# A Strassen mixture-of-experts kernel: second matmuls held back by three pieces, the even chunk split behind its silu, and the first expert's tokens transposed block by block

## The chip, the cores and the metric

The kernel runs on one core of a Trainium2 chip. The metric is the device time of one execution in microseconds (us); shorter is better. Engines are named as the profile names them: PE (matmul) with its weight loads PEld, DVE (vector), ACT (scalar), POOL (GpSimd) and SP (the engine that issues most DMAs).

## The reference

For 2048 tokens of width 512, the output is the input, plus a linear-attention block, plus a mixture of eight experts of which each token uses two:

```python
xn = _layernorm(x)
return x + _A_ref(xn, A_wqkv, A_wo) + _B_ref(xn, B_w_gate, B_w1, B_w2)

# _A_ref: 32 heads of width 16, no mask
pq, pk = phi(q), phi(k)                      # phi(t) = (t + 1 if t > 0 else exp(t)) + 1e-6
kv, z = sum over s of pk^T v, sum over s of pk
o = (pq @ kv) / (pq . z + 1e-6);  return o @ wo

# _B_ref: E = 8, F = 1792, K = 2
logits = xf @ w_gate;  gates = softmax(top-2 logits)
for e in range(E):
    h = silu(xf @ w1[e]) @ w2[e]
    out += w_e * h                            # w_e: the token's gate for e, or 0
```

## The kernel before

**Stages.** Until about 104 us the kernel normalises the 16 token tiles, transposes them and projects the keys. Until about 206 us it projects the queries tile by tile (`q_proj`, L1122), applies the attention of tiles 0 to 10 (`o_proj`, L1167) and, in between on DVE, computes the routing (`routing`, in slices that `piece` and the loop pull out of a generator). From 206 to 967 us it runs the experts. Last it applies the attention of the five remaining tiles and adds them to the output.

**Precision.** Each fp32 operand is split into a high part (ACT copies to fp32r, L111) and a low part (DVE subtracts, L114); each matmul then takes three passes (high x high, high x low, low x high). So a matrix that ACT or DVE produced can be used by PE only when ACT's high part is there, and for the other passes when DVE's low part is.

**Experts and pairs.** The experts are sorted by load: `r` is the place, with capacities of 576 to 512 tokens. An expert's tokens are gathered from DRAM by POOL in blocks of 128 (`gather1`, L901, tile `xg`), transposed by PE (`x_block`, L927, tile `xep`), copied by ACT (L934, tile `xr`) and split. The hidden width 1792 is cut into seven pairs `j` of two chunks of 128 (an even and an odd one). All pairs but the first two use a Strassen scheme, `pair_fast`: seven products p0 to p6 (L1071) of six matmuls each. p0, p2, p4 and p6 accumulate in one PSUM tile `px`, p1 and p3 in `pz`, p5 in `py`; after each product ACT or DVE reads the running sum. These tiles come from the tag `mm`, which has two buffers. p5 completes the even chunk: DVE adds (L1102), ACT applies silu (L1103), then `h_split` makes the high and the low part of `h`. p6 completes the odd chunk (silu at L1108).

**Second matmul.** `mm2` (L999 and L1002) multiplies a chunk of `h` with `w2`. One call, three matmuls, is a *piece*: one chunk into one accumulator `d`. For r = 0 to 4 there are six accumulators, d = 0 and 1 for 256 tokens at full width (L999, 512 columns) and d = 2 to 5 with the rest of the tokens transposed (L1002, 272 to 320 columns); for r = 5 to 7 (capacity 512, "single") there are four of 512 columns. The pieces of a pair are dealt out while the *next* pair runs: `fill(k)` puts some ahead of product k, `jobs(k)` issues the weight and token preparation behind it. Weight sums (L842 to L846, tile `wr`), their high parts (`ws`, `wa`, `w`) and the next expert's token sums (L945) all sit in `jobs`.

**Order of the work.** The order of every engine's queue is that in which the code issues it; nothing is reordered afterwards. `plan(g)` fills the slots, and its list `front` holds what goes between the first pieces of a pair: the next expert's `x_block`s (at j = 2, 3, 4) and the transposed outputs of the expert before (`y_out`, at j = 1 and 2).

Of the kernel before, what the change touches and what calls it, by code (L numbers as in the profile page):

```python
# [48 lines left out]
NPLAIN = 2  # L49
# [9 lines left out]
def linear_attn_plus_moe(  # L59
# [26 lines left out]
    def ta(name, w=D, dt=F32):  # L86
        t = wp.tile([P, DX if dt == F32 else 2 * DX], dt, tag="a", name=name, bufs=11)
        return t[:, :w]
# [34 lines left out]
    def load_x(t):  # L123
        xt[t] = ta(f"x{t}")
        Q.dma_start(xt[t], x[t * P:(t + 1) * P, :])
# [471 lines left out]
    def piece(n=1):  # L597
        for _ in range(n):
            next(side)
# [164 lines left out]
    def mid_b():  # L764
        kvs = kvw["s"]
        for i in range(2):
            M_v.append(hilo(tb, f"M{i}", 2))
        for g in range(4):
            mp = psm("acc", f"mp{g}")
            for i, (a, b) in enumerate(PASSES):  # L770
                T.matmul(mp, kvs[:, a, g * P:(g + 1) * P], wo_v[g // 2][b][:, g % 2, :],
                         start=(i == 0), stop=(i == 2))
            split(M_v[g // 2][0][:, g % 2, :], M_v[g // 2][1][:, g % 2, :], mp)
            if g % 2:
                for h in range(2):
                    Q.dma_start(M_d[g // 2, h].rearrange("p (k f) -> p k f", k=2), raw(M_v[g // 2][h]))
# [102 lines left out]
    def single(r):  # L879
        return CAP[r] == 4 * P  # L880
# [5 lines left out]
    def by_token(r):  # L886
        return [0, 1, 2, 3] if single(r) else [0, 1]
# [8 lines left out]
    def gather1(r, i):  # L896
        if i == 4 and single(r):
            return
        b = r * RB + i
        t = ta(f"xg{r}_{i}", DX)  # L900
        G.indirect_dma_start(out=t, out_offset=None, in_=xn_d,  # L901
                             in_offset=IOA(ap=gidx[:, b:b + 1], axis=0))
        xg[r, i] = t
# [61 lines left out]
    def h_split(r, n, hs):  # L965
        split(*hh[r, n], hs)
# [50 lines left out]
    def nacc(r):  # L1017
        return 4 if single(r) else 2 + KC

    def pieces(r, j):  # L1020
        e, o = 2 * j, 2 * j + 1
        n = nacc(r)
        if j < NP - 1:
            order = [(e, d) for d in range(n)] + [(o, d) for d in range(n)]
        else:
            order = [(e, 0), (e, 1), (e, 2), (o, 0), (o, 1), (o, 2)]
            order += [(c, d) for d in range(3, n) for c in (e, o)]
        return [lambda c=c, d=d: mm2(r, c, d) for c, d in order]

    def y_out(r, k, tag="mm"):  # L1030
# [28 lines left out]
    def pair_fast(r, j, fill, jobs):  # L1059
        n = half(r)  # L1060
        he, ho = h_tiles(r, j)
        c11, c12 = he[:, :n], he[:, n:]
        c21, c22 = ho[:, :n], ho[:, n:]

        def product(k, ps_, start):
            wn, xn_ = PRODUCTS[k]
            which, o = WPOS[wn]
            w, x = W1[r, j][which], XF[r, xn_]
            for kc in range(2):
                for i, (a, b) in enumerate(PASSES):  # L1070
                    T.matmul(ps_, w[a][:, o + kc, :], x[b][:, kc, :],  # L1071
                             start=(start and kc == 0 and i == 0), stop=(kc == 1 and i == 2),
                             skip_group_check=True)

        fill(0)
        px = psm("mm", f"px{r}_{j}", n)
        product(0, px, True)
        A.activation(c11, px, AF.Copy)  # L1078
        jobs(0)
        fill(1)  # L1080
        pz_ = psm("mm", f"pz{r}_{j}", n)
        product(1, pz_, True)
        A.activation(c22, pz_, AF.Copy)
        jobs(1)
        fill(2)
        product(2, px, False)
        A.activation(c12, px, AF.Copy)  # L1087
        jobs(2)
        fill(3)
        product(3, pz_, False)  # L1090
        V.tensor_tensor(c12, pz_, c12, op=ALU.add)  # L1091
        A.activation(c12, c12, AF.Silu)  # L1092
        jobs(3)
        fill(4)
        product(4, px, False)
        V.tensor_tensor(c22, px, c22, op=ALU.add)  # L1096
        A.activation(c22, c22, AF.Silu)  # L1097
        jobs(4)
        fill(5)
        pz_ = psm("mm", f"py{r}_{j}", n)  # L1100
        product(5, pz_, True)
        V.tensor_tensor(c11, pz_, c11, op=ALU.add)  # L1102
        A.activation(c11, c11, AF.Silu)  # L1103
        jobs(5)
        fill(6)
        product(6, px, False)
        h_split(r, 2 * j, he)
        A.activation(c21, px, AF.Silu)  # L1108
        jobs(6)
        h_split(r, 2 * j + 1, ho)  # L1110


    zt = ta("zt")
# [5 lines left out]

    eq = {}  # L1120

    def q_proj(t):  # L1122
        qp = psm("mm", f"qp{t}")
        for kc in range(KC):
            for i, (a, b) in enumerate(PASSES):
                T.matmul(qp, xT(t, a, kc), wq_v[kc // 2][b][:, kc % 2, :],
                         start=(kc == 0 and i == 0), stop=(kc == KC - 1 and i == 2))
        e = ta(f"e_q{t}")
        A.activation(e, qp, AF.Relu, scale=-1.0)
        A.activation(e, e, AF.Exp, scale=-1.0)  # L1130
        A.activation(e, e, AF.Identity, bias=eps6)
        eq[t] = (qp, e)

    def q_feat(t):
        qp, e = eq.pop(t)
        pq[t] = ta(f"pq{t}")
        V.scalar_tensor_tensor(pq[t], qp, 0.0, e, op0=ALU.max, op1=ALU.add)
        pz[t] = ta(f"pz{t}")
        G.tensor_tensor(pz[t], pq[t], zb, op=ALU.mult)
# [6 lines left out]
    def q_den(t):  # L1146
        dens[t] = wp.tile([P, H], F32, tag="den", name=f"den{t}", bufs=2)
        V.tensor_reduce(dens[t], heads(pz[t]), axis=AX.X, op=ALU.add)
# [67 lines left out]
    mid_lo(0)  # L1216
    mid_sum(1)
    mid_lo(1)
    q_proj(2)
    piece()  # L1220
    q_feat(1)
    mid_b()
    load_x(0)
    q_transp(0)
    q_den(1)
    q_norm(1)
    q_feat(2)
    q_proj(3)
    q_den(2)
    q_norm(2)  # L1230
    load_x(1)
# [4 lines left out]
    for t in range(OLAG + 1, NT - 2):  # L1236
        if t < NO + OLAG:
            o_out(t - OLAG - 1)
        spent = 0.0
        while spent < PERIOD:  # L1240
            c = next(side, None)
            if c is None:
                break
            spent += c
        q_den(t - 1)
        if 8 <= t < 11:
            fetch_w()
        q_proj(t)
        q_norm(t - 1)
        if t > NO:  # L1250
            pz_out(t - 1)
        q_feat(t)
        if t == 4:
            Q.dma_start(out[NO * P:S, :], x[NO * P:S, :])
        if t < NO + 2:
            load_x(t - 2)
            q_transp(t - 2)
        if t >= 11:
            plain_w()
        if t - OLAG < NO - 1:  # L1260
            o_proj(t - OLAG)
        while late:
            late.pop(0)()
        if t in (11, 12):
            gather1(0, 2 * t - 22)
            gather1(0, 2 * t - 21)
        if t == 13:
            gather1(0, 4)
            x_block(0, 0)
            x_block(0, 1)  # L1270


    t = NT - 2
# [1 line left out]
    q_proj(t)  # L1275
    q_norm(t - 1)
    pz_out(t - 1)
    x_block(0, 2)
    x_block(0, 3)
    q_feat(t)  # L1280
    q_proj(t + 1)
    x_block(0, 4)
    for name in ("B11", "B21", "B12", "B22"):
        x_hi(0, name)
        x_lo(0, name)
# [8 lines left out]
    def plan(g):  # L1294
# [48 lines left out]
            for k, f, name in steps.get(j, ()):  # L1343
                on(k, f, r + 1, name)
        if r > 0 and not single(r - 1):
            tg = "tr" if single(r) else "mm"
            for k in {1: (0, 1), 2: (2,)}.get(j, ()):
                front.insert(0 if j == 2 else len(front), lambda k=k: y_out(r - 1, k, tg))
        if j == 3 and r in (E // 2, E - 1):
            on(0, G.drain)  # L1350
        if r == E - 1:
# [9 lines left out]
                        front.append(lambda k=k: q_transp(NO + 2 * (j - 4) + k))  # L1361
        return at, front

    for g, (r, j) in enumerate(pairs):
        at, front = plan(g)
        todo = pieces(*pairs[g - 1]) if g else []
        rest = []
        if g == len(pairs) - 1:
            todo, rest = todo[:4], todo[4:]
        slots_ = 4 if g < NPLAIN else 7  # L1370
        total = len(todo)
        first = min(total, 2 + len(front)) if g >= NPLAIN else total // 4
        share = [first + (total - first) * k // (slots_ - 1) for k in range(slots_)]
        emitted = [0]

        def fill(k):
            while k == 0 and front:
                if emitted[0] < total:
                    todo[emitted[0]]()
                    emitted[0] += 1  # L1380
                front.pop(0)()
            while emitted[0] < share[k]:
                todo[emitted[0]]()
                emitted[0] += 1

        def jobs(k):
            for f in at[k]:
                f()

        (pair_plain if g < NPLAIN else pair_fast)(r, j, fill, jobs)  # L1390
        assert emitted[0] == total
        if g == 0:
            q_den(NT - 1)
            q_norm(NT - 1)
            pz_out(NT - 1)
# [83 lines left out]
```

## Time and profile before

| | |
|---|---|
| median of 3 runs | 988.62 us (986.51 to 989.22) |
| the profiled execution | 991.18 us, of which the instructions span 989.2 us |
| PE busy | 897.1 us (91% of the span) |
| DVE busy | 667.5 us (67%) |
| ACT busy | 550.3 us (56%) |
| POOL busy | 177.4 us (18%) |
| mean granted PE clock | 0.978 |
| DMA | 108.84 MB, mean 110 GB/s |

The profile gives for each engine when an instruction ran, how long the engine was idle before it and which engine's event ended that idle time. A row of the timeline reads: start, duration, engine, line, operation, tile written and tiles read, shape, count, and in brackets the idle time and its releaser. Matmuls are pipelined and their ends are modelled: the pace of PE is read from start to start, not from the durations. ACT and DVE rows overlap a little for the same reason.

### The profile page before, as it was taken

The numbers are of one execution on the slowest core, as the hardware profiler recorded it, in microseconds if no ns is written. First come the engines' busy times: TensorE is split into PE (matmuls) and PEld (weight loads), VectorE is DVE, ScalarE is ACT, GpSimd is POOL, SyncE is SP. The second block draws the span as 40 slices with busy tenths as digits, with TensorE's granted clock in tenths as the row PEclk, the third lists the DMA queues.
The fourth block names the chain that finished last, engine by engine and source line by source line (L and its number), as shares of the span: only waits on it lengthen the run. The fifth ranks groups of instructions, "written<-read, shape, count | busy, mean of one in ns | idle before, by whom it ended". The sixth has DMA issues, their size and how long they took to land. (4 is left out here: it accounts for less than half of the span.)

```text
span 989.2 us, 15229 instructions
## 1 busy us (share of the span) xinstructions
PE 897.1 (91%) x5582; PEld 790.4 (80%) x5582; DVE 667.5 (67%) x1441; ACT 550.3 (56%) x1191; POOL 177.4 (18%) x200
## 2 busy tenths in 40 slices
PE   9999999899898989998898889988888889889996
PEld 8899877678788878887888778877777777777785
DVE  7888789876675666657665775566667665766641
ACT  5665443555556655665655556555655555555540
POOL 2532143731004100410041003100400130020002
PEclk9999999999999999999999999999999999999999
DMA  5531164624226322632263226222632362256306
GB/s 171 171 129 43 57 212 133 200 87 128 86 69 134 114 86 80 144 91 85 86 136 101 77 85 159 79 75 75 161 97 66 87 157 67 83 116 204 117 1 151
DMA packets 71183, 108.84 MB, mean 110 GB/s; under 512 B 7618, under 2 KB 37570, under 8 KB 71074
## 3 DMA queue, kind: packets, MB, share of 16 engines
q1 hardware_dynamic: 62402, 87.82, 28.2%
q0 software_dynamic: 7840, 18.57, 9.8%
q10 hardware_dynamic: 864, 1.44, 0.4%
q8 instruction: 45, 0.74, 0.3%
q14 instruction: 32, 0.26, 0.1%
HBM read 85.89 MB, written 23.24 MB: 110 GB/s over the span
## 5 line engine op out<-in xcount | busy, mean ns | idle before, releaser
L976 POOL DMA_INDIRECT out_dram<-yo,sidx x37 | 58.4, 1579 | 637.3 <-DVE yo L974 577.2
L114 DVE TENSOR_TENSOR h<-hs,h 128x512 fp32r<-128x512 f32 (+5 forms) x112 | 79.6, 711 | 47.1 <-ACT h L111 46.3
L1091 DVE TENSOR_TENSOR hs<-pz,hs 128x256 f32<-128x256 f32 (+5 forms) x54 | 23.4, 434 | 91.7 <-PE pz L1071 86.6
L111 ACT ACTIVATE h<-hs 128x512 fp32r<-128x512 f32 (+5 forms) x112 | 70.9, 633 | 0.2
L1078 ACT ACTIVATE hs<-px 128x256 f32<-128x256 f32 (+5 forms) x54 | 21.1, 392 | 84.7 <-PE px L1071 84.7
L1103 ACT ACTIVATE hs<-hs 128x256 f32<-128x256 f32 (+5 forms) x54 | 23.0, 425 | 74.2 <-DVE hs L1102 74.2
L1092 ACT ACTIVATE hs<-hs 128x256 f32<-128x256 f32 (+5 forms) x54 | 23.0, 427 | 62.2 <-DVE hs L1091 62.2
L999 PE MATMUL y<-w_4h,h 128*128 128x512 f32 x88 | 39.6, 468 | 18.3 <-ACT h L111 17.3
L999 PE MATMUL y<-w_6h,h 128*128 128x512 f32 x88 | 36.3, 449 | 13.6 <-ACT h L111 13.5
L355 PE MATMUL gacc<-pkhl,xnhl 128*128 128x512 f32 x192 | 47.8, 397 | 0.0
L901 POOL DMA_INDIRECT xg<-xn_d,gidx x37 | 43.1, 1165 | 15.3 <-issue 8.3
L999 PE MATMUL y<-w_3h,h 128*128 128x512 f32 x88 | 35.5, 422 | 9.6 <-ACT h L111 9.5
L999 PE MATMUL y<-w_2h,h 128*128 128x512 f32 x88 | 35.8, 422 | 9.2 <-ACT h L111 9.0
L999 PE MATMUL y<-w_0h,h 128*128 128x512 f32 x88 | 35.3, 418 | 9.5 <-ACT h L111 8.5
L999 PE MATMUL y<-w_1h,h 128*128 128x512 f32 x88 | 35.7, 419 | 8.1 <-ACT h L111 8.0
L999 PE MATMUL y<-w_5h,h 128*128 128x512 f32 x88 | 34.6, 414 | 7.9 <-ACT h L111 7.7
L355 PEld LDWEIGHTS gacc<-pkhl,xnhl 128*128 128x128 f32 x192 | 34.9, 188 | 6.9 <-DVE pkhl L114 0.2
L999 PEld LDWEIGHTS y<-w_4h,h 128*128 128x128 f32 x88 | 18.0, 213 | 25.9 <-ACT h L111 19.0
L1087 ACT ACTIVATE hs<-px 128x256 f32<-128x256 f32 (+5 forms) x54 | 21.2, 392 | 26.1 <-PE px L1071 25.9
L999 PEld LDWEIGHTS y<-w_6h,h 128*128 128x128 f32 x88 | 17.7, 209 | 20.5 <-ACT h L111 15.0
L1097 ACT ACTIVATE hs<-hs 128x256 f32<-128x256 f32 (+5 forms) x54 | 22.9, 425 | 16.3 <-DVE hs L1096 15.0
L934 ACT ACTIVATE xr<-xep 128x256 f32<-128x256 f32 (+7 forms) x84 | 23.2, 338 | 15.5 <-PE xep L927 15.5
(517 smaller groups left out, 3162.9 us busy)
## 6 DMA issues: line engine op xcount, KB each, us to landing
wst<-in_B_w_dram SPq DMA_DIRECT2D x112, 512.0 KB, 3.8
x<-in_A_x_dram SPq DMA_DIRECT2D x27, 256.0 KB, 3.3
xn_d<-xn SPq DMA_DIRECT2D x16, 256.0 KB, 2.1
out_dram<-x SPq DMA_DIRECT2D x11, 256.0 KB, 2.3
out_dram<-zt SPq DMA_DIRECT2D x5, 256.0 KB, 4.2
out_dram<-in_A_x_dram SPq DMA_DIRECT2D x1, 1280.0 KB, 7.8
pz_d<-pz SPq DMA_DIRECT2D x5, 256.0 KB, 3.0
pzr<-pz_d SPq DMA_DIRECT2D x5, 256.0 KB, 4.1
```

The lines of the kernel that those rows point to most:

```text
L111: A.activation(hi, src, AF.Copy)
L114: V.tensor_tensor(lo, src, raw(hi), op=ALU.subtract)
L355: T.matmul(gacc[d], xnhl[:, a, d * P:(d + 1) * P], pkhl[:, b, :], start=(t == 0 and i == 0), stop=(t == NT - 1 and i == 2))
L901: G.indirect_dma_start(out=t, out_offset=None, in_=xn_d, in_offset=IOA(ap=gidx[:, b:b + 1], axis=0))
L934: A.activation(XR[r, f"B{q + 1}{c + 1}"][:, :, a - c * n:b - c * n], p[:, 2 * q:2 * q + 2, a - o:b - o], AF.Copy)
L976: st = G.indirect_dma_start(out=out, out_offset=IOA(ap=sidx[:w, b:b + 1], axis=0), in_=yo[:w], in_offset=None, compute_op=ALU.add).ins
L999: T.matmul(ya[r, d], h[a][:, d * P:(d + 1) * P], w[b][:, n % 2, :], start=(first and i == 0), stop=(last and i == 2))
L1087: A.activation(c12, px, AF.Copy)
L1091: V.tensor_tensor(c12, pz_, c12, op=ALU.add)
L1092: A.activation(c12, c12, AF.Silu)
L1097: A.activation(c22, c22, AF.Silu)
L1103: A.activation(c11, c11, AF.Silu)
```

## The change

There are five parts.

1. **Pieces held back.** The last three pieces of every pair are no longer issued in the next pair but at the head of the pair after that; the last pair keeps five. A pair now begins with the three held pieces instead of with pieces of the chunk that was just finished.
2. **Order of the accumulators.** The transposed accumulators come first, the token accumulators last.
3. **Split behind the silu.** `h_split` of the even chunk is issued directly behind its silu, ahead of `jobs(5)`; that of the odd chunk directly behind its silu, ahead of `jobs(6)`.
4. **First expert's tokens.** Block 0 is transposed an iteration earlier (at t = 12), block 2 ahead of tile 14's `q_proj`, block 4 ahead of tile 15's. The gathers stay where they were.
5. **Middle part.** The activations of `q_proj(2)` move behind `mid_b`, and one slice of the routing moves behind `q_proj(3)`. Besides, `y_out` always takes its PSUM tile from `mm` (before, from `tr` if the expert is single).

```diff
     def pieces(r, j):
         e, o = 2 * j, 2 * j + 1
-        n = nacc(r)
+        n, nt = nacc(r), len(by_token(r))
+        ds_ = [*range(nt, n), *range(nt)]
         if j < NP - 1:
-            order = [(e, d) for d in range(n)] + [(o, d) for d in range(n)]
+            order = [(e, d) for d in ds_] + [(o, d) for d in ds_]
...
         A.activation(c11, c11, AF.Silu)
+        h_split(r, 2 * j, he)
         jobs(5)
         fill(6)
         product(6, px, False)
-        h_split(r, 2 * j, he)
         A.activation(c21, px, AF.Silu)
+        h_split(r, 2 * j + 1, ho)
         jobs(6)
-        h_split(r, 2 * j + 1, ho)
...
-    q_proj(2)
-    piece()
+    q_proj(2, False)
     q_feat(1)
     mid_b()
+    q_exp(2)
...
     q_proj(3)
+    piece()
...
+        if t == 12:
+            x_block(0, 0)
         if t == 13:
             gather1(0, 4)
-            x_block(0, 0)
             x_block(0, 1)
+            x_block(0, 2)
...
-    x_block(0, 2)
     x_block(0, 3)
     q_feat(t)
+    x_block(0, 4)
     q_proj(t + 1)
-    x_block(0, 4)
...
-                front.insert(0 if j == 2 else len(front), lambda k=k: y_out(r - 1, k, tg))
+                front.insert(0 if j == 2 else len(front), lambda k=k: y_out(r - 1, k))
...
+    HELD = 3
+    rest = []
     for g, (r, j) in enumerate(pairs):
         at, front = plan(g)
-        todo = pieces(*pairs[g - 1]) if g else []
-        rest = []
-        if g == len(pairs) - 1:
-            todo, rest = todo[:4], todo[4:]
+        first = len(rest)
+        todo = rest + (pieces(*pairs[g - 1]) if g else [])
+        keep = HELD if g < len(pairs) - 1 else 5
+        todo, rest = todo[:len(todo) - keep], todo[len(todo) - keep:] if g else []
         slots_ = 4 if g < NPLAIN else 7
         total = len(todo)
-        first = min(total, 2 + len(front)) if g >= NPLAIN else total // 4
```

On PE, around the step from pair 4 to pair 5 of expert 3, this stood before (`y3_0` is accumulator 0 of expert 3, `h3_8` the even chunk of its pair 4, `px3_4` the end of the last product of pair 4, `px3_5` the first product of pair 5):

```order
L1071 MATMUL px3_4_6140<-xT4_3_5489,wa_3_4l_6005 128x264
L999 MATMUL y3_0_5659<-w2_3_4h_6178,h3_8_6105 128x512
L999 MATMUL y3_0_5659<-w2_3_4l_6179,h3_8_6105 128x512
L999 MATMUL y3_0_5659<-w2_3_4h_6178,h3_8_6105 128x512
L999 MATMUL y3_1_5672<-w2_3_4h_6178,h3_8_6105 128x512
L999 MATMUL y3_1_5672<-w2_3_4l_6179,h3_8_6105 128x512
L999 MATMUL y3_1_5672<-w2_3_4h_6178,h3_8_6105 128x512
L1071 MATMUL px3_5_6275<-xB11_3_4807,wa_3_5h_6149 128x264 x2
```

The changed kernel has at the same place, from the end of the first held piece on:

```order
L1002 MATMUL y3_5_5728<-h3_7_5950,w2_3_3l_6025 128x272
L999 MATMUL y3_0_5742<-w2_3_3h_6024,h3_7_5950 128x512
L999 MATMUL y3_0_5742<-w2_3_3l_6025,h3_7_5950 128x512
L999 MATMUL y3_0_5742<-w2_3_3h_6024,h3_7_5950 128x512
L999 MATMUL y3_1_5746<-w2_3_3h_6024,h3_7_5950 128x512
L999 MATMUL y3_1_5746<-w2_3_3l_6025,h3_7_5950 128x512
L999 MATMUL y3_1_5746<-w2_3_3h_6024,h3_7_5950 128x512
L1072 MATMUL px3_5_6269<-xB11_3_4798,wa_3_5h_6137 128x264 x2
L1072 MATMUL px3_5_6269<-xB11_3_4798,wa_3_5l_6138 128x264
L1072 MATMUL px3_5_6269<-xB11_3_4798,wa_3_5h_6137 128x264 x2
L1072 MATMUL px3_5_6269<-xB11_3_4798,wa_3_5l_6138 128x264
L1002 MATMUL y3_2_5690<-h3_8_6096,w2_3_4h_6169 128x272 x2
```

Between the last product of pair 4 and the first of pair 5 now stand three pieces of the odd chunk of pair 3 (`h3_7`); the new even chunk (`h3_8`) is first read behind p0 of pair 5.

On DVE, at the same step, this stood before (L1102 is the last add of the even chunk; `wr` are the weight sums of the pair after next, `xr4` and `xB22_4` the next expert's tokens, `h3_8` the low part of the even chunk):

```order
L1102 TENSOR_TENSOR hs3_4_6107<-py3_4_6232,hs3_4_6107 128x264
L845 TENSOR_TENSOR wr_3_6_6224<-wst53_6064 128x256
L846 TENSOR_TENSOR wr_3_6_6224<-wst53_6064,wr_3_6_6224 128x256
L945 TENSOR_TENSOR xr4_0_5830<-xr4_1_5831,xr4_0_5830 128x520
L114 TENSOR_TENSOR xB22_4_5829<-xr4_1_5831,xB22_4_5829 128x520
L114 TENSOR_TENSOR h3_8_6105<-hs3_4_6107,h3_8_6105 128x528
```

and now:

```order
L1103 TENSOR_TENSOR hs3_4_6098<-py3_4_6223,hs3_4_6098 128x264
L114 TENSOR_TENSOR h3_8_6096<-hs3_4_6098,h3_8_6096 128x528
L845 TENSOR_TENSOR wr_3_6_6215<-wst53_6055 128x256
L846 TENSOR_TENSOR wr_3_6_6215<-wst53_6055,wr_3_6_6215 128x256
L945 TENSOR_TENSOR xr4_0_5821<-xr4_1_5822,xr4_0_5821 128x520
L114 TENSOR_TENSOR xB22_4_5820<-xr4_1_5822,xB22_4_5820 128x520
```

The low part of `h` has moved ahead of four operations of `jobs(5)`. On ACT its high part has likewise moved ahead of one copy of `ws`.

On PE, at the first expert's tokens, this stood before (`qp13` is the query projection of tile 13, `op9` the output projection of tile 9, `xep0_0` the transpose of block 0 of expert 0):

```order
L1126 MATMUL qp13_2353<-wq1h_801,xnT13_130 128x512
L927 MATMUL xep0_0_2392<-ident_98,xg0_0_2283 128x128 x4
L927 MATMUL xep0_1_2402<-ident_98,xg0_1_2285 128x128 x4
L1126 MATMUL qp14_2414<-wq0h_721,xnT14_131 128x512
L1126 MATMUL qp14_2414<-wq0l_722,xnT14_131 128x512
```

and now:

```order
L1178 MATMUL op9_2332<-M1l_1647,pqT9_2261 128x512
L1178 MATMUL op9_2332<-M1h_1646,pqT9_2261 128x512
L927 MATMUL xep0_0_2355<-ident_98,xg0_0_2283 128x128 x4
L1127 MATMUL qp13_2369<-wq0h_721,xnT13_130 128x512
L1127 MATMUL qp13_2369<-wq0l_722,xnT13_130 128x512
```

Block 0 has moved ahead of the whole of `qp13`; blocks 1 and 2 stand behind it, 3 and 4 behind `qp14`, and none behind `qp15`.

More of the change, by code (lines that the diff above doesn't have):

```diff
@@ L1021, in pieces @@
         e, o = 2 * j, 2 * j + 1
-        n = nacc(r)
+        n, nt = nacc(r), len(by_token(r))
+        ds_ = [*range(nt, n), *range(nt)]
         if j < NP - 1:
-            order = [(e, d) for d in range(n)] + [(o, d) for d in range(n)]
+            order = [(e, d) for d in ds_] + [(o, d) for d in ds_]
         else:
-            order = [(e, 0), (e, 1), (e, 2), (o, 0), (o, 1), (o, 2)]
-            order += [(c, d) for d in range(3, n) for c in (e, o)]
+            order = [(e, d) for d in ds_[:3]] + [(o, d) for d in ds_[:3]]
+            order += [(c, d) for d in ds_[3:] for c in (e, o)]
         return [lambda c=c, d=d: mm2(r, c, d) for c, d in order]
@@ L1120, in linear_attn_plus_moe, with q_proj @@
     eq = {}
-    def q_proj(t):
+    def q_proj(t, act=True):
         qp = psm("mm", f"qp{t}")
@@ L1127, in q_proj, with q_exp @@
                          start=(kc == 0 and i == 0), stop=(kc == KC - 1 and i == 2))
+        eq[t] = qp
+        if act:
+            q_exp(t)
+    def q_exp(t):
+        qp = eq[t]
         e = ta(f"e_q{t}")
@@ L1345, in plan @@
         if r > 0 and not single(r - 1):
-            tg = "tr" if single(r) else "mm"
             for k in {1: (0, 1), 2: (2,)}.get(j, ()):
-                front.insert(0 if j == 2 else len(front), lambda k=k: y_out(r - 1, k, tg))
+                front.insert(0 if j == 2 else len(front), lambda k=k: y_out(r - 1, k))
         if j == 3 and r in (E // 2, E - 1):
```

## Prediction

> **What bounds the kernel now.** I read the clock of the core first, then the waits of PE, then stretches of the timeline.
>
> ```profile
> core 0: 989.2 us, clock 0.978
> ```
>
> The waits of PE (us in total, times, longest) name one cause above all: PE stands because the high part of a finished chunk `h` is not there.
>
> ```profile
> PE y L999 <- ACT h L111: 73.6, 53, 2.4
> PE y L999 <- DVE h L114: 1.7, 4, 0.9
> PE qp L1126 <- DVE pq L1137: 1.3, 1, 1.3
> ```
>
> So 75.3 us in 57 waits, about one for each of the 54 Strassen pairs. The real loss is larger, since ends of matmuls are modelled. PE's timeline in a pair of expert 7 shows by how much.
>
> ```profile
> 890.25 0.40 PE L999 MATMUL y<-w_0h,h 128*128 128x512 f32 x1
> 890.94 0.40 PE L1071 MATMUL pz<-xT,ws_1h 128*128 128x256 f32 x2
> 892.35 0.40 PE L1071 MATMUL px<-xT,ws_1h 128*128 128x256 f32 x2
> ...
> 898.57 0.28 PE L1071 MATMUL px<-xT,wa_1l 128*128 128x256 f32 x1
> 899.77 0.50 PE L999 MATMUL y<-w_1h,h 128*128 128x512 f32 x1 [0.92 <-ACT h L111]
> 901.53 0.40 PE L1071 MATMUL px<-xB,wa_2h 128*128 128x256 f32 x2
> ```
>
> Unhindered, a piece takes 890.94 - 890.25 = 0.69 us and a product with its piece 892.35 - 890.94 = 1.41, so a product 0.71 and one matmul of it 0.12. PE could have gone on at 898.69 and did at 899.77: 1.08 lost, where the view shows 0.92. The two pieces then took 1.76 instead of 1.39, as they wait again for DVE's low part. That makes 1.45 lost per pair, 0.5 more than shown.
>
> The third loss is the clock. Here are the longest kind of wait (expert 3, pair 4 to 5), then stretches with PE, PEld, DVE, ACT and POOL busy, granted clock and DMA.
>
> ```profile
> 563.47 0.78 PE L999 MATMUL y<-w_4h,h 128*128 128x512 f32 x1 [2.31 <-ACT h L111]
> 564.05 0.63 PE L999 MATMUL y<-w_4l,h 128*128 128x512 f32 x1
> 564.48 1.21 PE L999 MATMUL y<-w_4h,h 128*128 128x512 f32 x2
> ```
>
> ```profile
> 553.20:567.50 14.30, 11.99 (x74) 10.63 (x73) 10.35 (x20) 7.75 (x17) 0.00 (x0) 0.88 0.26 74
> 580.00:594.60 14.60, 12.66 (x80) 11.43 (x79) 9.40 (x18) 8.15 (x18) 0.00 (x0) 0.88 0.23 72
> 890.40:902.40 12.00, 11.08 (x68) 9.49 (x67) 7.51 (x15) 6.63 (x15) 0.09 (x1) 1.00 0.59 186
> 180.00:210.00 30.00, 25.44 (x121) 20.30 (x120) 20.14 (x38) 18.58 (x36) 16.82 (x14) 0.94 0.49 159
> 953.80:989.20 35.40, 27.94 (x151) 23.56 (x149) 8.50 (x15) 6.35 (x13) 6.36 (x7) 0.97 0.45 105
> ```
>
> Behind the 2.31 us wait matmuls of 512 columns start 0.43 us apart (564.48 - 564.05) instead of 0.23, and the clock of that pair is 0.88: 0.12 x 14.30 = 1.7 us of clock lost. Behind a wait of 0.92 it stays 1.00. In all, 0.022 x 989.2 = 21.8 us are lost; 1.8 of them lie in 180 to 210 us and 1.1 at the end. So about 19 us, eleven such stretches, belong to the experts. I count 1.5 us of time for each, 16 us, since PE does not work through all of a slow stretch.
>
> [...]
>
> **Held pieces and earlier split: what goes.** The chain to the wait, in another pair of expert 3 (DVE and ACT, and PE's last matmul of p6):
>
> ```profile
> 546.86 0.42 DVE L1102 TENSOR_TENSOR hs<-py,hs 128x264 f32<-128x264 f32 x1
> 547.20 0.41 DVE L845 TENSOR_TENSOR wr<-wst 128x256 f32<-128x256 f32 x1
> 547.31 0.28 PE L1071 MATMUL px<-xT,wa_3l 128*128 128x264 f32 x1
> 547.31 0.42 ACT L1103 ACTIVATE hs<-hs 128x264 f32<-128x264 f32 x1 [1.37 <-DVE hs L1102]
> 547.53 0.41 DVE L846 TENSOR_TENSOR wr<-wst,wr 128x256 f32<-128x256 f32 x1
> 547.65 0.61 ACT L111 ACTIVATE ws_5h<-wr 128x512 fp32r<-128x512 f32 x1
> 548.16 0.62 ACT L111 ACTIVATE h<-hs 128x528 fp32r<-128x528 f32 x1
> ...
> 549.49 0.63 ACT L111 ACTIVATE h<-hs 128x528 fp32r<-128x528 f32 x1
> 550.56 0.66 ACT L934 ACTIVATE xr<-xep 128x256 f32<-128x256 f32 x2 [0.44 <-PE xep L927]
> ```
>
> PE ends p6 at 547.43. Now the high part of `h` runs from 548.16 to 548.78; behind the silu it starts at 547.65 and is there at 548.2, the low part 0.65 later at 548.85. PE first does three held pieces (two of 0.69 and one of 272 columns, about 0.37: 1.75) and p0 (about 0.72) and asks at 549.9. So there is 1 us to spare in an ordinary pair, and all three losses go: 75.3 + 53 x 0.5 (26.5) + 16 = **118 us**.
>
> **What comes in their place.** First, the wait moves to p0 where a `front` uses `mm`. `xep` and `px` share two buffers, so p0 waits until ACT has copied the first block. ACT now does the odd chunk's `h` first and then the second `ws`, which needs DVE's sums (L845, L846). These stand behind the low part, so they end at 548.85 + 2 x 0.33 = 549.5; `ws` ends at 550.05 and `xr` (0.66) at 550.75. PE would reach p0 at 547.43 + 1.75 + two blocks of 0.4 (198.12 - 197.74 below) = 550.0. That is 0.8 us; two `y_out`s cost much the same. It happens at j = 3 and 4 of expert 0, j = 1 to 4 of experts 1 to 4 (18 times): 14 us, bounds 0 and 25 (1.4 each, if the second block's copy counts too).
>
> Second, DVE queues. The low part now waits about 1.0 us on DVE for silu and high part, with the sums, the token sums (L945) and the next pair's adds queued behind it, for which p5 and p6 wait (their buffers). DVE has 10.35 and 9.40 us of work in the two busiest kinds of pair (rows above), with this wait 11.4 and 10.4; PE without its losses needs 11.99 - 0.5 - 1.5 = 10.0 and 12.66 - 0.5 - 1.5 = 10.7. So DVE falls 1.4 behind in pair 4 and gains in pair 6. Since c11's add may come 1 us late and a `py` buffer over 2 us late (two pieces and p4 lie between), I take 1 us per expert, 7 us over seven experts; bounds 0 and 28 (4 each, if the odd chunk's wait of about 0.9 adds up over three pairs).
>
> The other edits of this part cost nothing: the accumulator order and the five pieces at the end keep PE's work the same, and the wait behind them stays covered by 5 x 0.69 us of pieces.
>
> **The first expert's tokens.** PE, POOL's gathers, and DVE's first use of block 4:
>
> ```profile
> 187.16 0.39 PE L1126 MATMUL qp<-wq0h,xnT 128*128 128x512 f32 x1
> 189.89 0.60 PE L927 MATMUL xep<-ident,xg 128*128 128x128 f32 x4
> 195.58 0.63 PE L927 MATMUL xep<-ident,xg 128*128 128x128 f32 x4 [1.26 <-DMA xg<-xn_d,gidx]
> 197.74 0.63 PE L927 MATMUL xep<-ident,xg 128*128 128x128 f32 x4 [1.53 <-DMA xg<-xn_d,gidx]
> 198.12 0.63 PE L1126 MATMUL qp<-wq0h,xnT 128*128 128x512 f32 x1
> 202.53 0.60 PE L927 MATMUL xep<-ident,xg 128*128 128x128 f32 x4
> 202.89 0.48 PE L1171 MATMUL op<-M0h,pqT 128*128 128x512 f32 x1
> 205.74 0.36 PE L1051 MATMUL hp<-xB,w_0h 128*128 128x288 f32 x1
> ```
>
> ```profile
> 182.51 1.97 POOL L901 DMA_INDIRECT xg<-xn_d,gidx  x1 [0.18 <-issue]
> 188.53 1.79 POOL L901 DMA_INDIRECT xg<-xn_d,gidx  x1
> 192.90 1.30 POOL L1139 TENSOR_TENSOR pz<-pq,zb 128x512 f32<-128x512 f32 x1 [0.23 <-DVE pq L1137]
> 194.34 1.79 POOL L901 DMA_INDIRECT xg<-xn_d,gidx  x1
> ...
> 200.68 0.16 DVE L938 TENSOR_TENSOR g<-xg,ohr 64x8 f32<-64x8 f32 x1 [1.62 <-DMA xg<-xn_d,gidx]
> ```
>
> Block 2 lands 7.0 us after its issue (195.5), block 4 6.3 after (200.6), so block 0 at about 189.5. The gathers are not moved, but PE now asks earlier: block 0 at 187.16 (wait 2.3). Then `qp13` (2.73) ends at 192.6, block 1 at 193.0, block 2 waits to 195.5, `qp14` ends at 198.6, block 3 at 199.0. Block 4's gather follows POOL's L1139, which follows `qp13`, now 2.7 later: issue 197.0, landing 203.3, 4.3 us of waiting. Behind it `qp15` and `op10` (2.85) end at 209.3 instead of 205.74: 3.6 us longer. Before, one slow stretch cost 4.41 - 2.73 = 1.7 there (198.12 to 202.53); now up to three waits can start one. I take **6 us**, bounds 3 and 9. DVE's small product of block 0 moves along and waits for the same landing, with the work for tile 13 behind it; that work follows `qp13` and so loses nothing more.
>
> [...]
>
> **The middle part.** Freeing `qp1`'s buffer ahead of the routing slice removes the 1.3 us wait above. The slice goes behind `q_proj(3)`, where 2.7 us of PE's work (a `q_proj`, above) cover it; without that cover the 1.3 us are spent again.
>
> **Sum.** 118 - 14 - 7 - 6 + 1 = 92 us less. The profiled execution is 991.18 us (span 989.2 and 2 around it), 2.6 above the median of the runs, 988.62. So it goes to 899, and the median to **897**.
>
> **Rivals.**
>
> 1. *DVE becomes the bound* in pairs 4 to 6: 28 us instead of 7, **918**. For it: 10.35 of work in a pair that PE could do in 10.0. Against: pairs 1 to 3 have slack, 7.51 in 12.00. Chance 0.14.
> 2. *The wait only changes its name*: p0 waits for ACT in every front, and ACT, late behind DVE, takes 2 us there: 18 x 2 = 36 instead of 14, **919**. For it: the shared buffers. Against: ACT is busy 7.75 of 14.30. Chance 0.12.
> 3. *The clock is not given back*, the 16 us stay: **913**. That would be so if the slow stretches had another cause than the waits for `h`; against it, 0.88 behind the long waits and 1.00 behind 0.92. [...] Chance 0.03.
> 4. *Slower than before: short waits throttle every pair.* If ACT's copies come so late that p2, p3 and p4 wait for `px` and `pz`, a pair has several short waits close together. [...] Against: after a product ACT has a product and a piece (1.41) for a copy of 0.4. Chance 0.04. [...]
>
> **Chances and range.** My forecast has 0.67. Its best case has none of the new waits in the experts and 3 us at the tokens: 118 - 3 + 1 = 116, 873. Bad, with 25, 14 and 9: 118 - 25 - 14 - 9 + 1 = 71, 918; rivals 1 and 2 with half of each other's cost reach 924. So 874 to 924. A change of 0.3% (3 us) is about what a measurement can tell. Faster 0.96 (the forecast and rivals 1 to 3), slower 0.03, same 0.01 (rival 4, whole or in part).
>
> **What would show it.** Right: the wait of `y` for `h` at L999 falls from 73.6 to under 8; the clock rises to 0.99 or more; expert 7's pairs take about 10.6 us instead of 12.00; `px` or `xep` appear with waits for ACT; the transposes of `xg` wait about 9 us instead of 2.8. Wrong: over 25 us of waits of PE for DVE at p5, p6 or `h` (rival 1), over 30 for ACT at p0 (rival 2), or a clock below 0.978 (rival 4).

## The result and the profile after

The changed kernel takes **906.29 us** (median of 4 runs, 905.53 to 907.18); the kernel before took 988.92 beside it. The ratio is 0.9169, with a 95% interval of 0.9151 to 0.9187. The profiled execution took 907.18 us.

The core's line, span and clock:

```profile
core 0: 905.5 us, clock 0.993
```

The waits of PE (us in total, times, longest) in the changed kernel:

```profile
PE yp L1037 <- DVE yt L1015: 6.8, 5, 1.5
PE px L1072 <- ACT xr L934: 4.3, 9, 0.5
PE xep L927 <- DMA xg<-xn_d,gidx: 4.3, 2, 2.5
PE py L1072 <- DVE hs L1092: 2.3, 5, 0.5
PE pqp L1167 <- POOL pz L1161: 2.2, 1, 2.2
PE px L1072 <- ACT yo L972: 2.0, 4, 0.5
PE xep L927 <- ACT e_q L1138: 1.8, 1, 1.8
```

The 75.3 us of waits of `y` for `h` are gone altogether, and nothing of that size has come in their place. The clock is 0.993 instead of 0.978. What is left is spread: `yp`, `px` and `py` lie in the experts, `xep` and `pqp` ahead of them.

To see where the time went, the span is cut at ACT's copies of p0: the stage from the copy of expert 0's pair 2 to that of the last pair. Window, length, then PE, PEld, DVE, ACT and POOL busy, clock, DMA. Before:

```profile
231.10:953.80 722.70, 647.44 (x4113) 574.78 (x4112) 464.36 (x953) 420.34 (x952) 82.63 (x92) 0.97 0.37 101
```

After (tokens of the first expert; the first two pairs; that stage; the end):

```profile
189.35:210.76 21.41, 15.35 (x69) 12.11 (x68) 9.87 (x23) 10.91 (x25) 10.44 (x8) 0.92 0.50 182
210.76:234.80 24.04, 21.94 (x146) 20.22 (x145) 22.96 (x39) 15.06 (x30) 13.73 (x12) 1.00 0.40 127
234.80:867.00 632.20, 614.96 (x4110) 560.90 (x4110) 459.39 (x956) 425.15 (x952) 81.36 (x90) 1.00 0.42 116
867.00:905.50 38.50, 29.88 (x160) 25.18 (x159) 8.51 (x15) 6.37 (x13) 6.38 (x7) 0.93 0.40 97
```

The stage fell from 722.7 to 632.2 us. I call its *unhindered pace* the sum over its matmuls, each counted with the median distance from start to next start that matmuls of its line and shape have in this stage: 605.3 us before and 603.3 after. So the losses fell from 117.4 to 28.9 us. The stage holds nearly the same matmuls in both kernels (4113 and 4110 in the rows above), so the difference of the two paces shows how exact this estimate is: to about 2 us. The first product of the experts (205.74 before) now starts 5.0 us later, at 210.76; the two pairs behind it are 1.3 shorter (25.4 before); the end is 3.1 longer (35.4 before). Together 90.5 - 5.0 + 1.3 - 3.1 = 83.7, which is the difference of the spans.

Two places show a good part of the 28.9. PE at the step from pair 0 to pair 1 of expert 5, and DVE beside it:

```profile
651.86 0.49 PE L1037 MATMUL yp<-ident,yt 128*128 128x128 f32 x3
653.86 0.33 PE L1037 MATMUL yp<-ident,yt 128*128 128x128 f32 x1 [1.50 <-DVE yt L1015]
```

```profile
652.10 0.69 DVE L114 TENSOR_TENSOR h<-hs,h 128x512 fp32r<-128x512 f32 x1 [1.15 <-ACT h L111]
652.71 0.42 DVE L845 TENSOR_TENSOR wr<-wst 128x256 f32<-128x256 f32 x1
653.04 0.42 DVE L846 TENSOR_TENSOR wr<-wst,wr 128x256 f32<-128x256 f32 x1
653.38 0.43 DVE L1015 COPY yt<-y 128x264 f32<-128x264 f32 x1
```

DVE stands 1.15 us at the low part of `h`, which the change put directly behind the silu, and the last accumulator's copy `yt`, for which PE waits, is queued three places behind it. The other place is p5 of pair 5, which waits about 0.5 us for the add at L1092 (the `py` row above): DVE again.

### The profile page after: what moved, and what is told of

The parts are those of the page before. It is cut to its first block, busy times and chain, and to the rows that moved or that the text cites. A ratio compares the mean times of both kernels' runs of the same rounds, so it can differ in the third digit from the quotient of the medians.

```text
span 905.5 us, 15239 instructions
## 1 busy us (share of the span) xinstructions
PE 866.7 (96%) x5582; PEld 777.3 (86%) x5582; DVE 662.5 (73%) x1441; ACT 555.5 (61%) x1191; POOL 178.7 (20%) x200
## 4 chain that ended last, share of the span: by engine, by line
PE 62%; DVE 20%; ACT 11%; issue 3%; DMA 2%; POOL 1%; DVEq 0%; ACTq 0%; another core or an unknown queue 0%; POOLq 0%
PE y L999 16%; PE px L1072 13%; PE pz L1072 7%; PE y L1002 6%; PE k L310 5%; ACT h L111 3%; PE qp L1127 3%; PE gacc L355 3%; PE op L1178 3%; PE py L1072 2%; DVE h L114 2%; DVE wr L843 1%; DVE xr L945 1%; ACT hs L1104 1%; DVE hs L1097 1%
## 5 line engine op out<-in xcount | busy, mean ns | idle before, releaser
L976 POOL DMA_INDIRECT out_dram<-yo,sidx x37 | 61.0, 1648 | 546.6 <-DVE yo L974 524.9
L114 DVE TENSOR_TENSOR h<-hs,h 128x512 fp32r<-128x512 f32 (+5 forms) x112 | 79.7, 712 | 73.1 <-ACT h L111 70.1
L1092 DVE TENSOR_TENSOR hs<-pz,hs 128x256 f32<-128x256 f32 (+5 forms) x54 | 23.3, 432 | 51.3 <-PE pz L1072 47.9
L1097 DVE TENSOR_TENSOR hs<-px,hs 128x256 f32<-128x256 f32 (+5 forms) x54 | 23.3, 432 | 26.0 <-PE px L1072 25.9
L1088 ACT ACTIVATE hs<-px 128x256 f32<-128x256 f32 (+5 forms) x54 | 21.1, 391 | 24.6 <-PE px L1072 24.5
L1136 ACT ACTIVATE e_q<-qp 128x512 f32<-128x512 f32 x16 | 9.6, 598 | 40.8 <-PE qp L1127 34.1
L999 PE MATMUL y<-w_6h,h 128*128 128x512 f32 x88 | 33.6, 402 | 0.0
L999 PE MATMUL y<-w_3h,h 128*128 128x512 f32 x88 | 32.5, 396 | 0.0
L999 PE MATMUL y<-w_4h,h 128*128 128x512 f32 x88 | 32.3, 394 | 0.0
L999 PE MATMUL y<-w_5h,h 128*128 128x512 f32 x88 | 31.6, 393 | 0.0
L927 PE MATMUL xep<-ident,xg 128*128 128x128 f32 x148 | 23.4, 282 | 6.7 <-DMA xg<-xn_d,gidx 4.3
L927 PEld LDWEIGHTS xep<-ident,xg 128*128 128x128 f32 x148 | 17.3, 142 | 14.1 <-ACT hs L1109 5.8
```

Of the source, the lines that this page charges most:

```text
L114: V.tensor_tensor(lo, src, raw(hi), op=ALU.subtract)
L927: T.transpose(p[:, kc * P:(kc + 1) * P], g[:, kc * P:(kc + 1) * P], ident)
L976: st = G.indirect_dma_start(out=out, out_offset=IOA(ap=sidx[:w, b:b + 1], axis=0), in_=yo[:w], in_offset=None, compute_op=ALU.add).ins
L999: T.matmul(ya[r, d], h[a][:, d * P:(d + 1) * P], w[b][:, n % 2, :], start=(first and i == 0), stop=(last and i == 2))
```

## Experiments

Ratios are to the kernel before; the intervals are 95%. "Stage" is the stretch defined above, set against its unhindered pace.

**Early split without held pieces.** The kernel before, with the two splits moved and nothing else:

```diff
         A.activation(c11, c11, AF.Silu)
+        h_split(r, 2 * j, he)
         jobs(5)
...
-        h_split(r, 2 * j, he)
         A.activation(c21, px, AF.Silu)
+        h_split(r, 2 * j + 1, ho)
         jobs(6)
-        h_split(r, 2 * j + 1, ho)
```

> The kernel before with the two splits behind their silus, and nothing else. Theory (PE waits for the high part of h, and the held pieces are what covers the chain): the high part comes 0.5 us earlier and the low part with it, so each of 53 waits loses about 0.5 of its 1.45 us (27 us), and the longest waits fall from 2.3 to 1.8 us, so that most of the eleven slow stretches of 1.5 us go (about 12 us): 945 to 958 us. Rival 1 (the split alone is the change): below 920 us. Rival 2 (DVE, now waiting 1 us for silu and high part in every pair, loses as much as PE gains): 980 to 990 us.

Measured: 956.53 us, 0.9679 (0.9641 to 0.9718), clock 0.989. The waits of PE:

```profile
PE y L999 <- ACT h L111: 49.3, 53, 2.0
```

By itself the early split is worth 32 us, as the theory had it: the longest cause of waiting shrinks from 73.6 to 49.3 us, but does not go.

**Held pieces without early split.** The changed kernel with both splits back where they were:

```diff
-        h_split(r, 2 * j, he)
         jobs(5)
         fill(6)
         product(6, px, False)
+        h_split(r, 2 * j, he)
         A.activation(c21, px, AF.Silu)
-        h_split(r, 2 * j + 1, ho)
         jobs(6)
+        h_split(r, 2 * j + 1, ho)
```

> The changed kernel with the two splits back at their old places. Theory: an ordinary pair has 1 us to spare, so there the late split costs nothing; at the end of pairs 4 and 6 the high part comes about as late as PE asks and the low part 0.9 us later: 14 places of about 0.8 us, less what DVE gains by not waiting for the silu: 908 to 918 us. Rival (both parts are needed, as the chain is longer than three pieces and a product): over 930 us.

Measured: **891.67 us**, 0.9019 (0.8983 to 0.9054). Both expectations missed: it is 14.6 us faster than the changed kernel. The stage:

```profile
237.60:854.60 617.00, 611.23 (x4110) 561.13 (x4110) 460.63 (x956) 410.88 (x953) 81.12 (x90) 1.00 0.43 119
```

617.0 us against the same pace of 603.3: a loss of 13.7 instead of 28.9. The waits for `yt` and at `py` are gone, those of `px` for `xr` are 2.1 instead of 4.3. So the split that helped the old order harms the new one. DVE in pair 1 of expert 4 shows how; the changed kernel, from the last add of the even chunk on:

```profile
580.41 0.41 DVE L1103 TENSOR_TENSOR hs<-py,hs 128x260 f32<-128x260 f32 x1
581.99 0.70 DVE L114 TENSOR_TENSOR h<-hs,h 128x520 fp32r<-128x520 f32 x1 [1.16 <-ACT h L111]
582.60 0.42 DVE L845 TENSOR_TENSOR wr<-wst 128x256 f32<-128x256 f32 x1
582.94 0.42 DVE L846 TENSOR_TENSOR wr<-wst,wr 128x256 f32<-128x256 f32 x1
```

The same pair with late splits:

```profile
573.93 0.42 DVE L1103 TENSOR_TENSOR hs<-py,hs 128x260 f32<-128x260 f32 x1
574.26 0.44 DVE L845 TENSOR_TENSOR wr<-wst 128x256 f32<-128x256 f32 x1
574.63 0.41 DVE L846 TENSOR_TENSOR wr<-wst,wr 128x256 f32<-128x256 f32 x1
575.88 0.70 DVE L114 TENSOR_TENSOR h<-hs,h 128x520 fp32r<-128x520 f32 x1 [0.84 <-ACT h L111]
```

Counted from the start of the add, the low part starts 1.58 us on with the early split and 1.95 with the late one: 0.37 gained. The second weight sum starts 2.53 us on instead of 0.70: 1.83 lost, with all that is queued behind it. Late, the two sums run in the time in which DVE would wait.

**First expert's tokens at their old places.** The changed kernel with the `x_block` calls back where they were (`h_split` early, as changed):

```diff
-        if t == 12:
-            x_block(0, 0)
         if t == 13:
             gather1(0, 4)
+            x_block(0, 0)
             x_block(0, 1)
-            x_block(0, 2)
...
+    x_block(0, 2)
     x_block(0, 3)
     q_feat(t)
-    x_block(0, 4)
     q_proj(t + 1)
+    x_block(0, 4)
```

> The changed kernel with the first expert's transposes where they were. Theory (PE asks for the blocks before the gathers have landed): the stretch from the output projection of tile 9 to the first product of the experts took 18.6 us before and takes 21.4 now, so 2.8 us come back: 903 to 904 us. Rival (the gathers' landing sets the end of that stretch either way): 905.5 to 907 us. Rival (the change hides transposes and only the slow stretch of the clock costs): 901 to 902.5 us if the slow stretch goes, over 907 if it stays.

Measured: 900.78 us, 0.9124 (0.9095 to 0.9152): 5.5 us faster than the changed kernel by the medians, 4.4 by the ratios. The waits of PE:

```profile
PE xep L927 <- DMA xg<-xn_d,gidx: 2.4, 3, 1.2
```

In the changed kernel the same transposes wait 1.75, 2.53 and 1.79 us (the last one put down to `e_q`, though block 4's gather lands there), 6.1 in all. The experts' first product starts 5.2 us earlier with the old places (205.51 against 210.76): 3.6 of that are these waits, and the rest is by my estimate clock: here matmuls of 512 columns start 0.23 us apart (199.36, 199.59, 199.82), where the changed kernel has a stretch of 3.4 us at 0.50 (197.3 to 200.7) and starts them 0.42 apart (198.94, 199.36). The theory on record (2.8 us) was too small; the prediction's 6 us for this part are near.

**Middle part as before.** The changed kernel with `q_proj(2)` and the routing slice back:

```diff
-    q_proj(2, False)
+    q_proj(2)
+    piece()
     q_feat(1)
     mid_b()
-    q_exp(2)
...
-    piece()
```

> The changed kernel with the activations of q_proj(2) and the routing slice where they were. Theory (the moved slice delays the denominators of tile 2, and PE waits 2.2 us for POOL at the transpose of tile 2 and runs a slow stretch behind it, against 1.3 us of waiting that went): 2.2 us come back: 903.5 to 904.5 us. Rival (the first expert's gathers take up what is won here): 905.5 to 907 us.

Measured: 906.89 us, 0.9184 (0.9152 to 0.9216): no difference. The waits of PE:

```profile
PE xep L927 <- DMA xg<-xn_d,gidx: 7.6, 3, 3.9
PE qp L1127 <- DVE pq L1144: 1.3, 1, 1.3
PE pqp L1167 <- POOL pz L1161: 0.2, 1, 0.2
```

The moved slice had put 2.2 us of waiting at `pqp` in place of 0.2, and taken 1.3 away at `qp`. What is won back there is lost again at the first expert's tokens. PE at block 4, and the window behind it:

```profile
202.68 0.63 PE L927 MATMUL xep<-ident,xg 128*128 128x128 f32 x4 [3.85 <-DMA xg<-xn_d,gidx]
```

```profile
203.60:207.00 3.40, 3.40 (x10) 2.61 (x9) 0.00 (x0) 0.19 (x2) 0.00 (x0) 0.51 0.00 0
```

Block 4's gather is issued 2.2 us earlier than in the changed kernel (196.78 against 198.94), and its transposes start 2.0 us earlier (202.68 against 204.67). But PE asks earlier still, waits 3.85 us instead of 1.79, and half clock follows, so that the experts' first product starts only 0.4 us earlier (210.32 against 210.76). The time is the rival's; the gathers' wait and the slow stretch behind it take up the gain together.

**Which of the two splits.** The changed kernel with only the odd chunk's split put back behind `jobs(6)`:

```diff
-        h_split(r, 2 * j + 1, ho)
         jobs(6)
+        h_split(r, 2 * j + 1, ho)
```

> The changed kernel with the odd chunk's split alone put back behind the last jobs of the pair; the even chunk is still split directly behind its silu. With both splits put back the time was 891.67 us, with both early 906.29. Theory: VectorE works in order, and it is the even chunk's split, standing there directly behind the addition of c11, that makes it stand idle for the silu and the high part (the changed kernel's trace has one such wait of 1.16 us in an ordinary pair, which in the kernel with late splits lies under the two additions of the next weights), so that all that follows on VectorE comes a microsecond late: this kernel keeps the loss, 903 to 909 us, and VectorE's wait for the high part of h stays near 70 us. Rival: the odd split, now ahead of the second weight sum's high part on ScalarE, delays the weights: then 889 to 895 us here. Second rival: both share it, 896 to 902.

Measured: 916.33 us, 0.926 (0.9233 to 0.9287), more than either had expected: slower by 10 than with both early. DVE's and PE's waits:

```profile
DVE h L114 <- ACT h L111: 86.6, 95, 1.2
```

```profile
PE px L1072 <- ACT xr L934: 9.2, 9, 1.1
PE px L1072 <- ACT yo L972: 4.1, 4, 1.1
```

And with only the even chunk's split put back:

```diff
-        h_split(r, 2 * j, he)
         jobs(5)
         fill(6)
         product(6, px, False)
+        h_split(r, 2 * j, he)
```

> The other half: the even chunk's split put back behind the seventh product, the odd chunk's split left ahead of the last jobs. Theory: the odd split has no loss of its own, 889 to 895 us, with VectorE's wait for the high part of h near 46 us as in the kernel with both splits late. Rival: the odd split carries the loss, 903 to 909 us. Second rival: they share it, 896 to 902.

Measured: 894.27 us, 0.903 (0.9003 to 0.9058), in time as the theory said, no different from both late. DVE's wait came out above the 46 us of the theory:

```profile
DVE h L114 <- ACT h L111: 54.5, 91, 1.5
```

So the even chunk's early split carries the loss. The extra 10 us with the odd one late were not foreseen. The waits point to ACT: the odd high part then stands behind the second `ws`, which waits for DVE's late sums, and the copies that free p0's buffer stand behind both. That is read from the waits and was not tried by itself.

**Only the low part late.** The changed kernel; ACT makes the even chunk's high part early, DVE its low part late:

```diff
-        h_split(r, 2 * j, he)
+        split_hi(hh[r, 2 * j][0], he)
         jobs(5)
         fill(6)
         product(6, px, False)
+        split_lo(*hh[r, 2 * j], he)
```

> The changed kernel with the even chunk's split cut in two: ScalarE makes its high part directly behind the silu, as the change has it, and VectorE makes its low part only behind the seventh product, as before the change. Theory: the loss of the early split is VectorE standing at the low part for the silu and the high part; ScalarE's early high part costs nothing: 889 to 896 us, with VectorE's wait for the high part of h below 55 us (70.1 in the changed kernel). Rival: the early high part holds up what follows it on ScalarE (the weights' high parts, the copies at the front of the next pair): 903 to 909 us.

Measured: 894.47 us, 0.9063 (0.9038 to 0.9089). DVE's wait:

```profile
DVE h L114 <- ACT h L111: 61.9, 88, 1.3
```

The time is as the theory said; the wait did not fall below 55. Moving one DVE instruction gives back 11.8 us by the medians, 10.5 by the ratios. The waits of PE at `yp` and `py` are gone with it; those of `px` for `xr` and `yo` stay (3.6 and 2.6 us). So what costs is not DVE's waiting in all (70.1 us against 61.9), but its waiting ahead of work that is ready and that PE needs soon.

**Held pieces, late splits, old token places** (the edits of the second and third experiment together):

> The changed kernel with both splits back at their old places and the first expert's token blocks back at theirs: the held pieces and the middle part are what is left of the change. Theory: the two losses lie in different stages and add, 14.6 us and 5.5 us: 906.3 - 20.1 = 886 us (884 to 889). Rival: part of the token loss was clock that other edits had lost, or the waits for the gathered rows come back elsewhere: then 889 to 892.

Measured: **884.77 us**, 0.8941 (0.8913 to 0.8968). The losses add up, as the theory had it.

**The same, with the middle part as before too:**

> As the run beside it, and the middle part put back as well: of the whole change only the held pieces and the order of the accumulators are left. Theory: with the tokens at their old places the gathers no longer take up what the middle part loses, so the wait of 2.2 us of the first matmul that reads POOL's product goes, and 1.3 us of the wait of a query product come back: about 1 us faster than the run beside it, 885 us (882 to 887). Rival: the middle part is worth nothing either way, within 1 us of the run beside it. Second rival: it was a gain that the moved tokens had hidden, then 2 us or more slower than the run beside it.

Measured: 885.62 us, 0.8942 (0.8915 to 0.897). The middle part is worth nothing either way; the first rival holds.

**How many pieces to hold.** Three more kernels differ from the one at 884.77 in one number, `HELD`. None:

```diff
-    HELD = 3
+    HELD = 0
```

> The fastest kernel so far (held pieces, late splits, old token places, 884.8 us) with no piece held back: each pair's first product then stands directly behind the last product of the pair before where no transpose is due, and its pieces begin behind it. Theory, from the trace of that kernel at one boundary: px comes free 1.37 us after the end of the seventh product and the low part of h is there 1.8 us after it; 22 boundaries without transposes lose 1.4 us for px and some 28 with transposes, which put a fresh piece first, lose 1.8: 30 + 50 = 80, and slow clock may come back: 955 to 985 us. Rival: the later place of the pieces behind the first product does it alone, and holding is worth little: 885 to 900.

Measured: 929.07 us, 0.9404 (0.9376 to 0.9432). Neither was right. Against the kernel before, about 59 us are gained without a single held piece. What this kernel still has of the change, beside the middle part that is worth nothing, is p0 standing ahead of the fresh pieces, the order of the accumulators and the PSUM tile of `y_out`; these were not tried apart. The theory's first term fell at a boundary without transposes; PE and ACT there:

```profile
714.45 0.28 PE L1072 MATMUL px<-xT,wa_4l 128*128 128x256 f32 x1
714.57 0.40 PE L1072 MATMUL px<-xB,wa_5h 128*128 128x256 f32 x2
...
715.10 0.61 ACT L111 ACTIVATE h<-hs 128x512 fp32r<-128x512 f32 x1
715.17 0.28 PE L1072 MATMUL px<-xB,wa_5l 128*128 128x256 f32 x1
715.62 0.36 ACT L1109 ACTIVATE hs<-px 128x256 f32<-128x256 f32 x1
715.76 0.50 PE L999 MATMUL y<-w_4h,h 128*128 128x512 f32 x1 [0.31 <-ACT h L111]
```

p0 of pair 5 (`wa_5`) starts 0.12 us behind p6 of pair 4, a microsecond before ACT reads p6's buffer: it has another one, `py`'s, and waits for nothing. What remains are the waits of `y` for `h` (25.3 us shown: 11.9 + 7.2 + 6.2 for DVE, ACT and ACT). The stage with none held, and with three for comparison:

```profile
229.90:890.60 660.70, 633.70 (x4110) 568.16 (x4110) 460.03 (x956) 417.44 (x952) 82.38 (x90) 1.00 0.40 112
```

```profile
228.50:845.40 616.90, 611.17 (x4110) 561.16 (x4110) 460.54 (x956) 410.70 (x953) 80.89 (x90) 1.00 0.41 119
```

It loses 57 us (660.7 against 603.7) instead of 14 (616.9 against 603.2); before the change it was 117.

One:

```diff
-    HELD = 3
+    HELD = 1
```

> The same kernel with one piece held back. A piece takes 0.70 us. Theory: 22 boundaries lose 1.37 - 0.70 = 0.7 us for px, some 28 lose 1.8 - 1.3 = 0.5 for the second piece, a fresh one, behind one held piece and one block's transposes: 15 + 14 = 29, so 905 to 918 us. Rival: one piece is cover enough, 884 to 890. Second rival: short waits at every boundary bring the slow clock back, over 930.

Measured: 895.59 us, 0.9071 (0.9043 to 0.9099), between the theory and its first rival; the clock stays at 0.998, so the second falls. The stage loses 24 us (626.9 against 603.4):

```profile
228.00:854.90 626.90, 615.83 (x4110) 564.76 (x4110) 459.66 (x956) 410.69 (x953) 84.57 (x90) 1.00 0.42 117
```

Four. The text on record below speaks of two held pieces, but the kernel that ran under this label held four; nothing had been written for four, and two were not measured:

```diff
-    HELD = 3
+    HELD = 4
```

> The same kernel with two pieces held back. Theory: two pieces are 1.40 us against 1.37 for px, and at boundaries with transposes the first fresh piece comes 2.6 us behind the seventh product against 1.8: nothing is lost, 884 to 888 us; the third piece is reserve. Rival: the reserve is needed where VectorE and ScalarE run late: 895 to 905.

Measured: **874.19 us**, 0.8849 (0.8821 to 0.8877), the fastest of all. The stage:

```profile
229.30:835.30 606.00, 605.98 (x4111) 563.49 (x4111) 460.41 (x956) 411.87 (x953) 80.19 (x90) 1.00 0.43 122
```

PE is busy for 605.98 of 606.00 us, and the stage is 2.6 us above the unhindered pace of 603.4. With three pieces PE still waited 2.1 us for `xr`, 2.0 for the low part of `h` and 1.1 for `yo`, none of which is left with four. So three pieces were not a reserve, but one too few: losses of 57, 24, 14 and 3 us for none, one, three and four. Five were not tried.

## Why the prediction was right, and where it was off

The forecast of 897 was 9 us too fast, and the result lies within its range. In the spans, 83.7 us went where its sum had 92.

1. *What goes, 118 us: right.* The stage lost 117.4 us before, by a count that does not use the prediction's terms. A pair of expert 7 takes 10.5 us (10.6 forecast), and the clock of the experts is back at 1.00 (0.97 before, by the rows of that stage). Rival 3, that the clock would not come back, fell.
2. *"So there is 1 us to spare in an ordinary pair, and all three losses go": the step that failed in part.* It put held pieces and early split into one sum. The first two parts of the change alone, held pieces and p0 ahead of the fresh ones, remove the waits of `y` for the high part of `h`; on top of them the early split costs 14.6 us. By the prediction's own rows it wasn't needed in an ordinary pair: without it the high part is there at 548.78, and PE asks at 549.9. The prediction saw the weight sums queued behind the low part, and did not set against it that the split could simply have stayed where it was. Nor did it ask what p0's new place does without held pieces: with none held the stage's loss falls from 117 to 57 us, and three held pieces take off 43 more.
3. *p0 at the fronts, 14 us: right in size, in part by luck.* Fourteen fronts (pairs 3 and 4 of expert 0, pairs 2 to 4 of experts 1 to 4) lose about 1 us each above the unhindered pace, 13.6 in all, of which the waits for `xr` and `yo` show 6.3. The prediction had 18 fronts at 0.8 us; at pair 1 p0 loses nothing, as PE has already waited there for `yt`. Rival 2's 36 did not come.
4. *DVE, 7 us: too small.* It is about 13.5: the add ahead of p5, which the prediction named, costs 6 (2.3 shown as waits), and the copies `yt` behind the delayed low part, which it did not name, cost 7.5 (6.8 shown) at five changes of expert. It stays inside its bounds of 0 and 28, and rival 1 came halfway. Of the 7.9 by which the forecast of the stage's new waits is too small (14 + 7 = 21 against 28.9) it holds 6.5: this is the term that was mis-sized.
5. *First expert's tokens, 6 us: near*, 4.4 to 5.5 by the third experiment, of which by my estimate 1.7 are clock (half of 3.4 us at 0.50). In the single profile the stretch grew by 2.8 only, as the kernel before had a slow stretch there too (0.50 from 198.3 to 201.7 us). The transposes wait 6.1 us, where the prediction expected about 9.
6. *Middle part, 1.3 us to the good: wrong.* "2.7 us of PE's work cover it" held for PE, but the slice stands in DVE's and POOL's way: `pqp` waits 2.2 us for POOL, and the wait for the gathers, with the clock behind it (3.85 us and then 0.51 in the fourth experiment), takes up what is gained or lost there.
7. *Left out:* the end grew by 3.1 us, part of which is work that the five last pieces moved behind the last copy of p0, and the first two pairs shrank by 1.3.

The points add up. Before rounding the sum was 118 - 14 - 7 - 6 + 1.3 = 92.3. The stage's new waits are 7.9 larger, and 0.6 less went (117.4 instead of 118); 2.0 come back because the unhindered pace comes out shorter; the first product starts 0.3 later than 6 - 1.3 would have it; the two pairs give 1.3, the end takes 3.1: 7.9 + 0.6 - 2.0 + 0.3 - 1.3 + 3.1 = 8.6, and 92.3 - 8.6 = 83.7. One sum of the prediction is loose: rivals 1 and 2 with half of each other's cost come to 922 and 926, and the 924 that it gives lies between them.

Rival 4, the slower case, fell clearly: without held pieces `y` waits 25.3 us in short pieces, none over 0.8 us, and the clock is 0.996.

## What to carry to other kernels

Two remedies for one wait don't add: here, work held back to cover a latency made hurrying the producer useless, and on DVE an instruction moved up to its producer, the low part of `h`, turned that latency into a standstill for all that was queued behind it: in the pair shown above 1.16 us, with L845 started 2.19 us behind the add instead of 0.33. Let such an instruction stand behind work that is ready anyway, and look at what stands behind it, not only at when its own result is there. And a cover is worth trying one size larger than the arithmetic asks for: the fourth held piece gave 9 to 11 us where no wait left in that stage was over 0.4.

## What the runs showed of the hardware

**The same wait, with half clock behind it and without.** In six kernels whose clock was read there, the wait at `pqp` is the same 2.16 to 2.19 us. From 134 to 138 us the mean granted clock is 0.73 in the changed kernel, 0.67 in that with held pieces and late splits, 0.78 in that with the old token places, 0.62 in that with both, and 1.00 in those with the low part late and with four held pieces. Two of them, first the changed kernel and then the one with four held pieces, with PE's row and stretches of 3.4 us:

```profile
135.51 0.86 PE L1167 MATMUL pqp<-ident,pz 128*128 128x128 f32 x4 [2.16 <-POOL pz L1161]
```

```profile
132.40:135.80 3.40, 1.24 (x8) 0.73 (x7) 3.26 (x10) 1.95 (x3) 1.33 (x2) 1.00 0.00 0
135.80:139.20 3.40, 3.40 (x12) 2.72 (x11) 3.13 (x12) 0.60 (x1) 1.00 (x1) 0.50 0.76 263
```

```profile
135.67 0.66 PE L1167 MATMUL pqp<-ident,pz 128*128 128x128 f32 x4 [2.16 <-POOL pz L1161]
```

```profile
131.60:135.00 3.40, 1.91 (x9) 1.23 (x7) 3.13 (x12) 1.39 (x3) 0.45 (x1) 1.00 0.00 0
135.00:138.40 3.40, 2.73 (x14) 2.34 (x15) 3.19 (x10) 1.16 (x2) 1.90 (x2) 1.00 0.22 80
```

In the traces of the kernel before and of the changed one, every slow stretch up to PE's last matmul, twelve and two of them, runs at 0.50 for 3.41 us, and their starts lie whole multiples of 3.41 us apart: 369.0, 467.9 and 495.2 us in the kernel before, for example, are 29 and 8 times that apart. In the changed kernel the wait lies within the 3.4 us ahead of such a stretch (PE is idle for 2.16 of them), and from 135.8 us on the clock is 0.50. In the kernel with four held pieces a cut at 135.0 us leaves 1.49 us of idle time ahead of it and 0.67 behind, and on both sides the clock is 1.00; whether the clock of that trace could have changed at 135.0 was not shown.

Cut at such multiples, the traces of the kernel before and of the changed one have 532 stretches of 3.41 us at full clock. Half clock followed 14 of them, in which PE was idle for 1.63 to 2.62 us; in the 518 others it was idle for at most 1.79. In the kernel before, half clock followed the stretch from 194.9 to 198.3 us, where PE was idle for 2.2 us, 1.53 in one wait and 0.7 in another. Whether executions of one kernel differ in this way was not tried.
